# A fused attention and MLP kernel, forward and backward: the gradient over w1 for batch 0 moved from VectorE rows to TensorE columns, and the second pass begun two rows earlier

## The chip, the cores and the metric

The kernel runs on one core of one Trainium2 chip. The time is the device time of an execution in microseconds (us), the median of three runs. All matrices are bf16, and sums are kept in fp32.

## The reference, cut to what matters

One decode step of a transformer layer with a batch of two, and its gradient for every input:

```
x, grad_out: [2, 1, 640]     k_cache, v_cache: [2, 32, 4096, 128]
wq: [640, 4096]   wo: [4096, 640]   w1: [640, 1728]   w2: [1728, 640]

q  = layernorm(x) @ wq                      # 32 heads of 128
p  = softmax(q k^T * 128**-0.5);  o = p v
h  = x + o @ wo
h2 = h + relu(layernorm(h) @ w1) @ w2       # the output
outputs: h2, and the gradients of x, k_cache, v_cache, wq, wo, w1, w2 for grad_out
```

The caches are read, and gradients of their size are written: 64 K tiles and 64 V tiles of 1 MB come in, V comes in once more for the backward pass, and 128 tiles of 1 MB go out.

## The kernel before, in words

**Rows.** The program is written out by hand in one order (`tc.manual_schedule()`, L62): each engine executes its instructions in the order in which Python emits them. The outer loop (L1238) goes over `plan`; one iteration is called a row here, and row i handles pair i of 64 pairs (batch, head). H is 32, so rows 0 to 31 are batch 0.

**First pass.** `p1_iter(i)` (L468) is one row in eight steps k = 0 to 7: TensorE transposes the K tile of pair i (L440), scores come from one-column products (L453), the pair before it is scaled by its softmax weights on VectorE (`pk_half`, L486), and the V tile of the pair before that is multiplied (`m_part`, L476). So K tile i is read in rows i and i+1, V tile i in row i+2.

**Second pass.** `p2_iter(j)` (L884) makes the gradients of one pair's K and V and stores them, from a V tile called W. From row `P2_AT` on, every second row of the first pass carries one second-pass pair as well, and after row 65 only second-pass work is left. `P2_AT = H + 2 + M0_ITERS` (L1174); `M0_ITERS` is 7, so it is row 41. The first six pairs keep their V tile from the first pass.

**The middle.** Rows 34 to 40 lie between the end of batch 0's first pass and the first row of the second pass. There `middle_gen(0)` (L768) runs beside the first-pass rows of batch 1, as a generator that `bg_step` (L1155) advances by a credit in each step k. It needs the whole of batch 0 and yields what the second pass of batch 0 needs: the attention output through wo (`a_group`, L621), a layer norm, the 70 one-column products with w1 (`hf_ps`, L794), the gradient `ghfc` of the hidden values, and then the gradient over w1. For that, ghfc is spread over the partitions (`spread_some`, L655: a transpose for each chunk of 128 into PSUM and a copy on ScalarE), and VectorE multiplies and sums 15 pieces of w1 with it (`ttr`, L693, called at L816: five pieces of 640 columns, five of 640, five of 448). `turn()` (L699) lets at most five of these into a row. Then come the layer norm's gradient (`ln_bwd`) and the first heads of `go_group` (L708). In rows 34 to 40 `pk_act` (L491) also moves six of 32 scalings of a row to ScalarE.

**Loads.** All loads of the first pass stand in one list, `queue` (L1189), and go out in its order on SyncE's (SP's) DMA queue: K of row i, V of row i-2, and at rows named in `W_AT` (L1190) and `W2_AT` the four parts of wo, w1 (2160 KB, the fifth entry, row 35) and the three tiles of w2. `pump()` (L1205) is called in every step and issues as far as free buffers reach. A cache tile needs one of 13 buffers of 1 MB (`take("ld", ...)`, L90); each comes back with `give` when its tile has been read. w2's tiles hold buffers until `ga_gen` (L836) has used them, up to row 28. The last six pairs of batch 0 keep their V tile, so that from row 28 a row gives back one buffer and not two. w1 has a home of its own (`w1_t`, L343).

**The scratch around it.** `wide_row` (L648) is one row of 1280 columns that several steps use in turn. `later_heads()` (L651) is the part of the stored softmax weights that batch 1's last heads will fill, used as scratch until then. All small PSUM results share bank 7 (`mid`, `bc`, L71).

Of the kernel before, what the change touches and what calls it, by code (L numbers as in the profile page):

```python
# [7 lines left out]
FP32 = mybir.dt.float32  # L8
BF16 = mybir.dt.bfloat16
ALU = mybir.AluOpType  # L10
ACT = mybir.ActivationFunctionType
AX = mybir.AxisListType
# [3 lines left out]
def kernel(  # L16
# [20 lines left out]
    nc = tc.nc  # L37

    B, Sq, D = A_x.shape
    _, H, Sk, Dh = A_k_cache.shape  # L40
# [3 lines left out]
    ND = D // 128  # L44
# [3 lines left out]
    NF = NFF + (1 if F_rem else 0)  # L48
# [9 lines left out]
    def f_kc(c):  # L58
        return 128 if c < NFF else F_rem
# [7 lines left out]
    small = ctx.enter_context(tc.tile_pool(name="small", bufs=3))  # L67
# [5 lines left out]
    def pst(shape, dtype, role, name):  # L73

        k = banks[role].pop(0)
        banks[role].append(k)
        return ps.tile(shape, dtype, tag=f"bank{k}", bufs=1, name=name)
# [12 lines left out]
    def take(tag, shape, name):  # L90
        assert free[tag] > 0, (tag, name)
        free[tag] -= 1
        k = homes[tag].pop(0)
        stored.discard(k)
        t = pools[k].tile(shape, BF16, tag=f"big{k}", bufs=1, name=name)
        home_of[id(t)] = (tag, k, t)
        return t
# [9 lines left out]
    def give(t, to=None, out=False):  # L107
        tag, k, _ = home_of.pop(id(t))
        if out:
            stored.add(k)  # L110
        to = to or goes_to(tag)
        owned[tag] -= 1
        owned[to] += 1
        free[to] += 1
        homes[to].append(k)
        given_at[k] = step[0]
# [42 lines left out]
    ident_bf = const.tile([128, 128], BF16)  # L159
# [205 lines left out]
    FP = 6  # L365
# [51 lines left out]
    u4 = [None]  # L417
# [214 lines left out]
    def a_heads(i):  # L632

        if a_next[0] < o_next[0]:
            a_group()
        elif o_next[0] < NP1 // OG and i >= o_next[0] * OG + OG + 2:
            b, g = divmod(o_next[0], H // OG)
            if b > 0 or i >= W_AT[g * OG * 4 // H] + 4:
                o_group()
# [8 lines left out]
    def wide_row(name):  # L648
        return cols.tile([128, B * D], BF16, tag="wide_row", name=name)

    def later_heads():  # L651

        return P_bf[:, B * H - D // NSC:, :].rearrange("p h s -> p (h s)")

    def spread_some(colsrc, c0, n, kc_of, dst):  # L655

        t = pst([128, D], BF16, "bc", "bcb_ps")
        w = 0
        for c in range(c0, c0 + n):
            kc = kc_of(c)  # L660
            nc.tensor.transpose(t[:, w:w + kc], colsrc[0:kc, c:c + 1].to_broadcast([kc, 128]), ident_bf[0:kc, 0:kc])
            w += kc
        nc.scalar.copy(out=dst[:, 0:w], in_=t[:, 0:w])
        return w
# [19 lines left out]
    def store_rows(cols_bf, out_ap):  # L684
# [5 lines left out]
        nc.vector.tensor_copy(out=r[0:n, :], in_=t[0:n, :])  # L690
        nc.sync.dma_start(out=out_ap.rearrange("b s (c p) -> (b s c) p", p=128), in_=r[0:n, :])

    def ttr(in0, in1, acc, width, junk, kc=128):  # L693
        nc.vector.tensor_tensor_reduce(out=junk[0:kc, 0:width], in0=in0, in1=in1, scale=1.0, scalar=0.0,  # L694
                                       op0=ALU.mult, op1=ALU.add, accum_out=acc)
# [3 lines left out]
    def turn():  # L699

        while slot[0] <= 0:
            yield 0.0
        slot[0] -= 1

    def one(src, b):
        return src[:, :, b]
# [34 lines left out]
    def mlp_out():  # L741
# [23 lines left out]
        store_rows(y_bf, out_0)  # L765
        yield

    def middle_gen(b):  # L768
        if o_next[0] < (b + 1) * H // OG:
            o_group()  # L770
        u4[0] = wide_row("u")[:, 0:256].bitcast(FP32)
        nc.vector.tensor_reduce(out=u4[0], in_=u_bank[0][:].rearrange("p (s d) -> p d s", s=4),
                                axis=AX.X, op=ALU.add)
        yield
        while a_next[0] < (b + 1) * H // OG:
            if a_next[0] == o_next[0]:
                o_group()
                yield
                yield
            a_group()  # L780
            yield
        at_bf = small.tile([128, ND], BF16, tag="at_bf", bufs=1, name="at_bf")
        nc.vector.tensor_copy(out=at_bf[:], in_=asum[:, b, :])
        nc.vector.tensor_tensor(out=h1c[:, :, b], in0=xg32[:, b, :], in1=at_bf[:], op=ALU.add)
        h32 = small.tile([128, 1, ND], FP32, tag="h32", bufs=1, name="h32")
        nc.vector.tensor_copy(out=h32[:, 0, :], in_=h1c[:, :, b])
        yield ("a", b)
        u_out(b)
        yield from ln_fwd(h32[:], 1, x2c[:, :, b:b + 1], rstd2[:, b:b + 1])
        hf_ps = pst([128, NF], FP32, "mid", "hf_ps")  # L790
        for cf in range(NF):
            kc = f_kc(cf)
            for c in range(ND):
                nc.tensor.matmul(hf_ps[0:kc, cf:cf + 1], lhsT=w1_t[:, c, cf * 128:cf * 128 + kc],  # L794
                                 rhs=x2c[:, c, b:b + 1], start=(c == 0), stop=(c == ND - 1))
            yield 0.25
        nc.vector.tensor_scalar(out=acol[:, 0:NFF, b], in0=hf_ps[:, 0:NFF], scalar1=0.0, scalar2=None, op0=ALU.max)
        if F_rem:
            nc.vector.tensor_scalar(out=acol[0:F_rem, NFF, b:b + 1], in0=hf_ps[0:F_rem, NFF:NF],
                                    scalar1=0.0, scalar2=None, op0=ALU.max)  # L800
        mask = small.tile([128, NF], FP32, tag="mask", bufs=1, name="mask")
        nc.vector.tensor_single_scalar(out=mask[:], in_=acol[:, :, b], scalar=0.0, op=ALU.is_gt)
        nc.vector.tensor_tensor(out=ghfc[:, :, b], in0=ga[:, b, :], in1=mask[:], op=ALU.mult)
        yield from wait(3)
        fbc = wide_row("fbc")
        gx2 = small.tile([128, 1, ND], FP32, tag="gx2", bufs=1, name="gx2")
        gx2p = small.tile([128, ND, 3], FP32, tag="gx2p", bufs=1, name="gx2p")
        first_f = 0
        for k, n in enumerate((ND, ND, NF - 2 * ND)):
            row = fbc[:, (k % 2) * D:(k % 2 + 1) * D]  # L810
            w = spread_some(one(ghfc, b), k * ND, n, f_kc, row)
            yield
            for c in range(ND):
                yield from turn()
                part = w1_t[:, c, first_f:first_f + w]
                ttr(part, row[:, 0:w], gx2p[:, c, k:k + 1], w, part if b else later_heads())  # L816
                yield 0.85
            first_f += w
        nc.vector.reduce_sum(out=gx2[:, 0, :], in_=gx2p[:], axis=AX.X)
        yield ("w1", b)  # L820
        yield from ln_bwd(gx2[:], x2c[:, :, b:b + 1], rstd2[:, b:b + 1], gc[:, :, b:b + 1], gh1c[:, :, b:b + 1], 1)
        row = wide_row("hbc")
        hbc, junk = row[:, 0:D], row[:, D:2 * D]
        spread_some(one(gh1c, b), 0, ND, lambda c: 128, hbc)
        yield
        yield ("gh1", b)

        first = H - KEPT[b]
        bounds = [(first, first + 2), (first + 2, H)] if b == 0 else [(first, H)]
        bounds += [(h, min(first, h + GH)) for h in range(0, first, GH)]  # L830
        for h0, h1 in bounds:
            yield from go_group(b, h0, h1, hbc, junk)
        if b > 0:
            yield from mlp_out()
# [335 lines left out]
        forced[0] = False  # L1170

    EARLY = 2
    M0_ITERS = 7
    P2_AT = H + 2 + M0_ITERS  # L1174
    RATES = (0.2, 0.8, 0.2, 0.8, 0.45)
    RATE2 = 0.65
# [10 lines left out]


    queue = []  # L1189
    W_AT = (10, 15, 20, 24, 35)  # L1190
    W2_AT = (8, 13, 18)
    for n, (ii, jj) in enumerate(plan):
        if ii is not None:
# [11 lines left out]
    def pump():  # L1205
        while queue:
            what, k = queue[0]
            if what == "w":
                load_weights(k)
            else:  # L1210
                tag = "ld"
                if free["ld"] < 1 or (alone[0] and not ready("ld", 13)):
                    return
                if what == "w2":
                    w2_tiles[k] = load_w2(k, tag)
                else:
                    load_tile(what, k, tag)
            queue.pop(0)
# [19 lines left out]
    for n, (i, j) in enumerate(plan):  # L1238
# [57 lines left out]
        for k, _ in enumerate(p1_iter(i, i < H + 1, 0)):  # L1296
            for _ in range(at.get(k, 0)):
                if g2 is not None:
                    p2_step()
            if k == 5 and not H + 2 < i < P2_AT + 6:  # L1300
                a_heads(i)
            pump()

            spread[0] = 1 if i < P2_AT else 2
            at_k[0] = k
            if i >= P2_AT:
                slot[0] = int(k == 6 or (k == 1 and j is not None))
            elif i > H + 1:
                slot[0] = {1: 2, 3: 1, 4: 1, 6: 1}.get(k, 0)
            else:  # L1310
                slot[0] = int(k in (1, 6))
            bg_step(0, rate)
            bg_step(1, 0.0)
# [43 lines left out]
```

## Time and profile before

| | |
|---|---|
| median of 3 runs | 891.27 us (886.06 to 891.39) |
| profiled execution, its own time | 890.14 us |
| its span (first to last instruction) | 888.4 us |
| mean granted TensorE clock | 0.766 |
| busy: TensorE matmul, VectorE, ScalarE, GpSimd | 739.3, 680.5, 497.9, 170.9 us |
| moved by DMA | 361.86 MB, mean 407 GB/s over the span |
| read from HBM, written to it | 211.11 MB, 149.13 MB |
| a K or V tile from issue to landing, median | 17.3 us, 15.6 us |

The page cuts the span in 40 slices of 22.2 us; a digit is a share in tenths. A line of the view by windows names a stretch in us from the span's start, then its length, the busy time and instruction count of each engine in it, the granted clock of TensorE, the share of the 16 DMA engines' time in use, and the GB/s that they moved. PE is TensorE's matmul, PEld its weight loads, DVE is VectorE, ACT ScalarE, POOL GpSimd, SPq SyncE's DMA queue. In the profile w1 and w2 both appear under the name `w_t`, with the line telling them apart. The start of row i is the first K transpose of pair i on TensorE.

### The profile page before, as it was taken

Reading aid. Unit: us, or ns where it says so; the run is one execution under the profiler, and the core shown is the slowest. Engines: PE = TensorE matmul, PEld = TensorE weight load, DVE = VectorE, ACT = ScalarE, POOL = GpSimd, SP = SyncE. Lnnn points to the kernel's source line nnn. Section 1 sums busy time; section 2 is a strip of 40 time slices with the busy share of each in tenths; the row PEclk is TensorE's granted clock in tenths of the full one; section 3 lists DMA queues with packets and bytes.
Section 4 is the critical chain, followed back from the end, with each engine's and each line's share of the span. In section 5 each row is a group of like instructions: output and inputs, shape, how many; then the busy total and the mean of one; then the engine's idle time right before and its main releaser. Section 6 shows DMA issues by size and latency. Waiting matters only on the chain.

```text
span 888.4 us, 24848 instructions
## 1 busy us (share of the span) xinstructions
PE 739.3 (83%) x10143; PEld 618.9 (70%) x10143; DVE 680.5 (77%) x1281; ACT 497.9 (56%) x1292; POOL 170.9 (19%) x291
## 2 busy tenths in 40 slices
PE   4999899899999998987967887878876899967870
PEld 4887788789887887876757776656666667654550
DVE  2666788677788797885878898778878789989660
ACT  1444343345777665654635878777656766646660
POOL 1344433343212000000011101111001011211010
PEclk9999999899999998998995555555556755555655
DMA  9999999999879999999999999999999999999995
GB/s 379 425 419 415 417 409 417 426 423 388 312 301 401 418 422 426 422 425 426 421 392 394 416 422 424 425 425 425 426 425 411 424 425 414 425 427 424 424 424 230
DMA packets 56035, 361.86 MB, mean 407 GB/s; under 512 B 5681, under 2 KB 11505, under 8 KB 15217
## 3 DMA queue, kind: packets, MB, share of 16 engines
q1 hardware_dynamic: 46968, 303.29, 82.4%
q0 software_dynamic: 8912, 56.97, 15.6%
q8 instruction: 80, 1.31, 0.5%
q14 instruction: 35, 0.28, 0.1%
q10 hardware_dynamic: 40, 0.01, 0.0%
HBM read 211.11 MB, written 149.13 MB: 406 GB/s over the span
## 4 chain that ended last, share of the span: by engine, by line
PE 36%; DMA 32%; DVE 16%; ACT 9%; issue 4%; SPq 0%; DVEq 0%; ACTq 0%; POOL 0%; POOLq 0%
PE t_ps L440 15%; DMA Vt<-in_A_v_cache_dram 13%; DMA out_dram<-gV 12%; PE m_ps L476 9%; DMA out_dram<-gK 6%; DVE gK L860 5%; ACT gV L950 4%; DVE gV L860 4%; PE s_ps L453 3%; DVE pk L486 3%; PE u_ps L514 2%; ACT t_sb L445 2%; PE dp_ps L453 2%; DMA Kt<-in_A_k_cache_dram 2%; DVE hbc L694 2%
## 5 line engine op out<-in xcount | busy, mean ns | idle before, releaser
L445 ACT COPY t_sb<-t_ps 128x512 f32<-128x512 f32 x479 | 273.0, 587 | 197.3 <-PE t_ps L440 193.0
L453 PEld LDWEIGHTS <-t_sb 128*128 128x128 bf16 x4096 | 179.7, 103 | 57.9 <-ACT t_sb L445 30.4
L440 PE MATMUL t_ps<-ident_f,Wt 128*128 128x128 f32 x832 | 199.9, 391 | 1.5 <-ACT t_sb L445 1.5
L486 DVE TENSOR_TENSOR pk<-Kt,ep 128x2048 bf16<-128x2048 bf16 (+1 forms) x128 | 152.7, 1193 | 49.1 <-ACT ep L540 30.6
L476 PE MATMUL m_ps<-pk,Vt 128*128 128x129 bf16 x2048 | 172.4, 223 | 20.6 <-DMA Vt<-in_A_v_cache_dram 19.4
L860 DVE TENSOR_TENSOR gK<-rb,gsp 128x2048 bf16<-128x2048 bf16 x128 | 152.9, 1223 | 20.9 <-DMA out_dram<-gV 16.4
L476 PEld LDWEIGHTS <-Vt 128*128 128x128 bf16 x2048 | 125.9, 99 | 51.7 <-issue 29.0
L440 PEld LDWEIGHTS t_ps<-ident_f,Wt 128*128 128x128 f32 x832 | 138.9, 203 | 29.8 <-issue 21.8
L440 PE MATMUL t_ps<-ident_f,Kt 128*128 128x128 f32 x1024 | 154.8, 284 | 3.8 <-DMA Kt<-in_A_k_cache_dram 3.2
L860 DVE TENSOR_TENSOR gV<-rb,pp 128x2048 bf16<-128x2048 bf16 (+1 forms) x128 | 143.2, 1144 | 18.5 <-DMA out_dram<-gV 13.3
L440 PEld LDWEIGHTS t_ps<-ident_f,Kt 128*128 128x128 f32 x1024 | 113.0, 144 | 6.4 <-ACT t_sb L445 2.7
L502 POOL COPY pk<-ep 128x16 bf16<-128x16 bf16 x80 | 84.5, 1058 | 160.9 <-ACT ep L540 79.3
L453 PE MATMUL dp_ps<-gom,t_sb 128*128 128x2 bf16 x2048 | 96.3, 168 | 19.6 <-ACT t_sb L445 19.1
L453 PE MATMUL s_ps<-qm,t_sb 128*128 128x2 bf16 x2048 | 87.4, 164 | 1.5 <-DVE t_sb L443 1.5
L1004 ACT CAST ot<-o_ps 128x512 bf16<-128x512 f32 (+3 forms) x152 | 67.4, 492 | 6.7 <-PE o_ps L998 4.2
L604 ACT CAST MT<-m_ps 128x128 bf16<-128x128 f32 x64 | 17.0, 265 | 95.2 <-PE m_ps L476 95.1
L905 POOL COPY pp<-P_bf 128x64 bf16<-128x64 bf16 x64 | 34.1, 536 | 127.7 <-DVE gV L860 125.0
L903 ACT ACTIVATE rb<-dp_ps,rt 128x256 bf16<-128x256 f32 x64 | 30.2, 472 | 42.3 <-PE dp_ps L898 41.5
L694 DVE CUSTOM_DVE_ANT_0 hbc<-wo_t,hbc 128x640 bf16<-128x640 bf16 x64 | 52.8, 826 | 0.3
L694 DVE CUSTOM_DVE_ANT_0 gxj<-wqs,gqr 128x1024 bf16<-128x1024 bf16 x40 | 48.8, 1220 | 0.2
L950 ACT ACTIVATE gV<-rb,pa 128x128 bf16<-128x128 bf16 x152 | 46.5, 394 | 0.0
L440 PE MATMUL t_ps<-ident_f,Vt 128*128 128x128 f32 x192 | 40.4, 351 | 1.8 <-ACT t_sb L445 1.8
(208 smaller groups left out, 710.7 us busy)
## 6 DMA issues: line engine op xcount, KB each, us to landing
Kt<-in_A_k_cache_dram SPq DMA_DIRECT2D x64, 1024.0 KB, 17.3
Vt<-in_A_v_cache_dram SPq DMA_DIRECT2D x64, 1024.0 KB, 15.6
Wt<-in_A_v_cache_dram SPq DMA_DIRECT2D x52, 1024.0 KB, 17.0
out_dram<-gK SPq DMA_DIRECT2D x48, 1024.0 KB, 17.4
out_dram<-gV SPq DMA_DIRECT2D x47, 1024.0 KB, 17.9
out_dram<-gV POOLq DMA_DIRECT2D x17, 1024.0 KB, 9.7
out_dram<-gK POOLq DMA_DIRECT2D x16, 1024.0 KB, 10.2
wq_t<-in_A_wq_dram SPq DMA_DIRECT2D x5, 1024.0 KB, 6.8
```

The costliest lines, as they stand in the source:

```text
L440: nc.tensor.transpose(t_ps[:, j, :], natf[:, 2 * cc:2 * cc + 2, :].rearrange("p c k -> p (c k)"), ident_f[:])
L445: nc.scalar.copy(out=t_sb[:], in_=t_ps[:])
L453: nc.tensor.matmul(dst[:, sc:sc + 2], lhsT=v[:, j, :, par], rhs=vecs[:, par, :], start=(par == 0), stop=(par == 1))
L476: nc.tensor.matmul(r["m"][:, 0:129], lhsT=r["V"][:, sc, :], rhs=r["pk"][sc // HALF][:, sc % HALF, 0:129], start=(sc == 0), stop=(sc == NSC ...
L486: nc.vector.tensor_tensor(out=p["pk"][k][:, 0:n, 0:128].rearrange("p s (a two) -> p s a two", two=2), in0=p["K"][:, sl, :].rearrange("p s ...
L502: nc.gpsimd.tensor_copy(out=col, in_=e)
L694: nc.vector.tensor_tensor_reduce(out=junk[0:kc, 0:width], in0=in0, in1=in1, scale=1.0, scalar=0.0, op0=ALU.mult, op1=ALU.add, accum_out=acc)
L860: nc.vector.tensor_tensor(out=pairs_view(dst[:, sl, :]), in0=row.rearrange("p (a two) -> p a two", two=2)[:, None, :, :].to_broadcast([128 ...
L903: nc.scalar.activation(out=rb[:], in_=bank[:, 128:384], func=ACT.Copy, scale=rt[:, b, h:h + 1])
L905: nc.gpsimd.tensor_copy(out=pp[:], in_=P_bf[:, b * H + h, :, None].to_broadcast([128, NSC, 2]))
L950: nc.scalar.activation(out=gV[:, NSC - act + k, :], in_=c["rb"][:, 0:128], func=ACT.Copy, scale=pa[:, k:k + 1])
L1004: nc.scalar.copy(out=ot[0:P, k, n0:n0 + nn], in_=o_ps[0:P, 0:nn])
```

## The change

Four things are done together.

1. **w1 is loaded at row 12.** The fifth entry of `W_AT` becomes 12. Since loads run ahead, its DMA is issued behind K tile 12 and V tile 10, in row 7.
2. **w1 is transposed on TensorE.** From row 14 on, at the end of a row (k = 7), `w1_transpose` takes one of w1's 14 chunks of 128 hidden columns: five 128x128 transposes into bank 7 and one copy of 640 columns on ScalarE. Chunks 0 to 5 and 6 to 11 go to two of the 13 `ld` buffers (taken in rows 14 and 20), chunk 12 to `later_heads()` and chunk 13 to a `wide_row`; these last two wait until `ga` is done and come in rows 29 and 30.
3. **Batch 0's gradient over w1 is 70 one-column products** (`gx_by_chunks`) with the transposed w1, summed in PSUM; the two `ld` buffers are then given back, in row 36. Batch 1 keeps the old way (`gx_by_rows`, the removed lines moved there).
4. **`M0_ITERS` is 5.** The middle is rows 34 to 38, and the second pass begins at row 39.

```diff
+    w1T = {"next": 0, "tiles": []}
+    def w1T_chunk(cf):
+        if cf < 2 * FP:
+            return w1T["tiles"][cf // FP][:, cf % FP, :]
+        return later_heads() if cf == 2 * FP else w1T["row"][:, D:2 * D]
+    def w1_transpose():
+        cf = w1T["next"]
+        if cf >= 2 * FP:
+            if "ga" not in done:
+                return
+            if cf > 2 * FP:
+                w1T["row"] = wide_row("u")
+        elif cf % FP == 0:
+            w1T["tiles"].append(take("ld", [128, FP, D], "w1T"))
+        kc = f_kc(cf)
+        t = pst([128, D], BF16, "mid", "w1T_ps")
+        for c in range(ND):
+            nc.tensor.transpose(t[0:kc, c * 128:(c + 1) * 128], w1_t[:, c, cf * 128:cf * 128 + kc], ident_bf[:])
+        nc.scalar.copy(out=w1T_chunk(cf)[0:kc, :], in_=t[0:kc, :])
+        w1T["next"] = cf + 1
+    def gx_by_chunks(b, gx2):
+        t = pst([128, ND], FP32, "mid", "gx_ps")
+        for c in range(ND):
+            for cf in range(NF):
+                kc = f_kc(cf)
+                nc.tensor.matmul(t[:, c:c + 1], lhsT=w1T_chunk(cf)[0:kc, c * 128:(c + 1) * 128],
+                                 rhs=ghfc[0:kc, cf, b:b + 1], start=(cf == 0), stop=(cf == NF - 1))
+            yield 0.5
+        for w in w1T["tiles"]:
+            give(w)
+        nc.vector.tensor_copy(out=gx2[:, 0, :], in_=t[:])
...
-        for k, n in enumerate((ND, ND, NF - 2 * ND)):
-            row = fbc[:, (k % 2) * D:(k % 2 + 1) * D]
-            w = spread_some(one(ghfc, b), k * ND, n, f_kc, row)
-            yield
-            for c in range(ND):
-                yield from turn()
-                part = w1_t[:, c, first_f:first_f + w]
-                ttr(part, row[:, 0:w], gx2p[:, c, k:k + 1], w, part if b else later_heads())
-                yield 0.85
-            first_f += w
+        if b == 0:
+            yield from gx_by_chunks(b, gx2)
+        else:
+            yield from gx_by_rows(b, gx2)
...
-    M0_ITERS = 7
+    M0_ITERS = 5
+    W1T_AT = 14
...
-    W_AT = (10, 15, 20, 24, 35)
+    W_AT = (10, 15, 20, 24, 12)
...
+            if k == 7 and W1T_AT <= i < H and w1T["next"] < NF:
+                w1_transpose()
```

## The prediction

> **What bounds the kernel now.** I read the page's slices first, then the view by windows cut at the rows, then SyncE's and TensorE's timelines around the middle.
>
> ```profile
> PEclk9999999899999998998995555555556755555655
> DMA  9999999999879999999999999999999999999995
> GB/s 379 425 419 415 417 409 417 426 423 388 312 301 401 418 422 426 422 425 426 421 392 394 416 422 424 425 425 425 426 425 411 424 425 414 425 427 424 424 424 230
> ```
>
> DMA is full in nearly every slice. The bytes, 361.86 MB, are the same after the change, so the time moves only with DMA time that is left unused. Apart from start and tail there is one large hole: slices 10 to 13 (388, 312, 301, 401), the middle. Cut at the rows (first line rows 12 to 25, second rows 26 to 33, third rows 34 to 42):
>
> ```profile
> 81.07:169.52 88.45, 80.85 (x1370) 70.08 (x1367) 67.44 (x134) 33.64 (x102) 33.20 (x44) 0.96 1.02 416
> 169.52:212.64 43.12, 43.12 (x763) 38.18 (x760) 32.35 (x59) 18.93 (x58) 19.31 (x23) 1.00 1.01 422
> 212.64:271.28 58.64, 57.63 (x984) 50.80 (x981) 48.27 (x138) 44.73 (x132) 14.21 (x33) 0.97 0.83 316
> ```
>
> Rows 12 to 25 take 6.3 us each and TensorE has 7.6 us to spare in them: they wait for tiles. Rows 26 to 33 have TensorE busy throughout, 5.4 us each. In rows 34 to 42 DMA moves 316 GB/s against 423 when full: 58.64 x (1 - 316/423) = 14.8 us are lost there. Row by row (34 to 42):
>
> ```profile
> 212.64:218.88 6.24, 6.24 (x121) 5.78 (x118) 5.08 (x20) 4.67 (x15) 2.51 (x6) 1.00 0.90 363
> 218.88:226.04 7.16, 7.16 (x166) 6.51 (x162) 4.87 (x19) 4.96 (x17) 1.91 (x6) 1.00 0.97 363
> 226.04:233.29 7.25, 7.25 (x100) 6.52 (x97) 4.09 (x12) 4.93 (x13) 1.71 (x4) 0.76 0.71 293
> 233.29:238.79 5.50, 5.50 (x100) 4.88 (x97) 5.43 (x13) 4.89 (x15) 1.42 (x4) 1.00 0.70 253
> 238.79:244.96 6.17, 5.87 (x99) 4.88 (x97) 6.10 (x17) 4.97 (x17) 2.02 (x4) 1.00 0.90 340
> 244.96:251.03 6.07, 5.92 (x103) 5.12 (x100) 5.32 (x19) 5.10 (x18) 1.14 (x4) 1.00 0.96 368
> 251.03:257.09 6.06, 5.91 (x101) 5.15 (x98) 5.21 (x16) 4.91 (x14) 1.52 (x5) 1.00 0.91 341
> 257.09:265.56 8.47, 8.11 (x137) 7.15 (x134) 7.80 (x19) 5.26 (x14) 0.70 (x1) 1.00 0.52 204
> 265.56:271.28 5.72, 5.67 (x103) 4.82 (x100) 4.39 (x9) 5.03 (x16) 1.26 (x1) 1.00 1.01 352
> ```
>
> Engines, not DMA, set these rows: TensorE is busy for almost all of each, VectorE for 5.43 of 5.50 and 6.10 of 6.17 us in rows 37 and 38, where most of the 15 pieces lie. A row of the first pass asks for two tiles of 1.05 MB, 4.96 us at 423 GB/s, and takes 5.5 to 7.3 us.
>
> SyncE's timeline shows what fills part of that hole now: w1.
>
> ```profile
> 202.08 0.43 SPq L363 DMA_DIRECT2D w_t<-in_B_w_dram  x1
> 208.06 0.33 SPq L461 DMA_DIRECT2D Kt<-in_A_k_cache_dram  x1
> 212.81 0.33 SPq L461 DMA_DIRECT2D Vt<-in_A_v_cache_dram  x1
> 218.97 0.33 SPq L461 DMA_DIRECT2D Kt<-in_A_k_cache_dram  x1
> ```
>
> It goes out at 202.08, when loads have already thinned to one tile in 5 to 6 us (208.06, 212.81, 218.97), because the kept V tiles hold buffers. So w1's 2.21 MB travel almost free of charge.
>
> **The change part by part.** The end of the hole is a state: the row from which DMA is full again, row 43 before (420 GB/s), row 41 after. By the built program's order both have the same K and V tiles asked for relative to the row, so the changed kernel reaches it with two rows' loads, 4.19 MB, not yet made. These cost 4.19/0.423 = 9.9 us later, where DMA is full. The result is therefore: change of row 34's start, plus the time of rows 34 to 40 after, minus the 58.64 us, plus 9.9 us.
>
> *w1 at row 12.* It now travels among rows 12 to 25, which wait for tiles, and holds each later tile back by 2.21 MB: 2.21/0.423 = 5.2 us. It is issued behind K tile 12 and V tile 10 on SyncE, and K tile 13 and all behind it wait. The end of that stretch is a V tile's landing (row 25 lasts 9.76 us for it), so row 26 starts 5.2 us later; rows 26 to 33 are TensorE's and keep their length. Bounds: 0, if the later rows make it up (K tile 34 lands 8.9 us before row 34), and 5.3 at 416 GB/s. I take 5.2, since lead that row 26 lacks can't shorten TensorE-bound rows.
>
> *70 transposes, 14 copies.* No transpose of w1 is in the trace; the nearest are five 128x128 bf16 ones before a copy:
>
> ```profile
> 229.50 0.61 PE L661 MATMUL bcb_ps<-ident_bf,ghfc 128*128 128x128 bf16 x5
> 229.95 0.40 PE L476 MATMUL m_ps<-pk,Vt 128*128 128x129 bf16 x4
> ```
>
> The next matmul starts 0.45 us after them, so 0.45 us per chunk. Twelve chunks (5.4 us) fall in rows 14 to 25, under TensorE's 7.6 us of waiting plus 5.2 us that w1 adds; without this cover they would cost up to 5.4 us. Two fall in rows 29 and 30: +0.9 us. The copies (0.69 us each, as L663's) are ScalarE work beside 33.64 busy of 88.45 us: nothing; a copy late in a row can hold the next row's transposes by some 0.3 us, under the same cover. Bank 7 is shared with `a_group`, whose sum VectorE reads within its row: nothing.
>
> *Two `ld` buffers fewer, rows 14 to 36.* A tile goes out one row closer to its use. In the built order K tile 36 and V tile 34 leave at the end of row 34 and are read from row 36's start; before, the same tiles left two rows or more ahead. The lead is row 35 (about 7.2 us) for K and about 7.7 us for V. The landings of these stretches:
>
> ```profile
> DMA to landing us min/median/max: 6.4/13.0/16.5
> ...
> DMA to landing us min/median/max: 7.2/8.3/15.2
> ```
>
> (K from 186 to 262 us, V from 190 to 290 us.) Where the queue is nearly empty I take the lower ends, so rows 36 and 37 wait 0 to 0.6 us for V; 0 in the sum, the rest in the range. In row 36 two buffers come back at once and four loads leave together.
>
> *70 products for 15 pieces.* The twin of the new products is L794:
>
> ```profile
> 223.19 0.89 PE L794 MATMUL hf_ps<-x2c,w_t 128*128 128x1 bf16 x30
> 223.94 0.63 PE L476 MATMUL m_ps<-pk,Vt 128*128 128x129 bf16 x8
> ```
>
> 30 in 0.75 us before the next starts, 25 ns each: 70 cost TensorE 1.8 us, in row 36. Removed there are five spread transposes (0.45 us) and later nine more, three copies, and on VectorE 10 x 0.82 + 5 x 0.62 = 11.3 us:
>
> ```profile
> L694 DVE CUSTOM_DVE_ANT_0 P_bf<-w_t,fbc x15: 608/812/840, 230.9 to 247.2; 128x640 bf16<-128x640 bf16 x10, 128x448 bf16<-128x448 bf16 x5
> ```
>
> Rows 37 and 38 thus fall from VectorE to TensorE's own pace.
>
> *Rows 34 to 40 after.* Row 34 and 35 as now, 6.24 and 7.16. Row 36: 5.4 us (a row that TensorE sets) plus 1.8 for the products, nothing for a cold clock (0.76 in row 36 now): 7.2. Row 37: layer norm's gradient and one spread, 5.4 + 0.5 = 5.9. Row 38: the first two heads, as row 40 now, 6.0. Rows 39 and 40, the first of the second pass, as 41 and 42 now, 8.47 and 5.72. Sum 46.7. Bounds: 40.2 with the five middle rows at the shortest row, 5.21; 49.9 with rows 36 to 38 at 7.25 each.
>
> *Sum.* 5.2 + 0.9 + 46.7 - 58.64 + 9.9 = +4.1 us on the profiled execution's 890.14: 894.2. That execution lies 1.1 us under the median, less than the runs differ among themselves; I give 894. Afterwards nothing gets shorter: the second pass moves the same bytes at 420 to 427 GB/s.
>
> **The rivals.**
>
> *A. w1 stays hidden.* Row 34 starts as now, because lead over TensorE makes the 5.2 us up. For it: rows 26 to 33 wait for no tile. Against: TensorE is the limit in them, so they can't run faster to make anything up. It gives 894.2 - 5.2 = 889.0, still within 1%; with the middle rows at their floor too (46.7 to 40.2), 882.5. That is about the most that the middle can give.
>
> *B. The two buffers are missed* (slower by over 1%). Place: V tiles of rows 36 and 37, one row ahead. It sets in when a V tile takes over 7.7 us to land; at 11.5 us (between 8.3 and the 15.2 that a full queue showed) two rows wait 3.8 us each, 7.6 in all, 901.8; at 15.2 it is 15 us, 909. The limit of 900.2 is crossed from about 10.7 us. For it: landings over 13 us are common in this stretch. Against: those belong to a queue with many tiles in it, and here two would be in it. The Trainium skill, "DMA: Bandwidth & Descriptors", section "Anatomy of one DMA", gives 2.0 us plus bytes over 436 GB/s for one DMA (on GpSimd's path; these leave from SyncE): by that a tile lands in 4.4 us and B can't occur. The trace does not agree, its shortest K landing here is 6.4 us, so B keeps a chance.
>
> *C. The middle doesn't fit in five rows*, and the first second-pass row runs what is left in one lump. By the built order both first heads are done in row 38, so this doesn't happen; were one row short, it costs about a row, 6 us: 900.
>
> **How the numbers follow.** About 1% (8.9 us) is what a measurement of this kernel can tell from no change: 882.4 to 900.2 counts as within 1%. The forecast, a loss of some 4 us between -1 and +8: 0.56. A: 0.22, of which half its way to the floor, 0.11, is faster by over 1% or at its edge. B: 0.17, and C with unforeseen waits 0.05; of these 0.20 end over 900.2. So faster 0.11, within 1% 0.69, slower 0.20. The range leaves out the last of A and the far half of B: 882 to 905. The likeliest case alone: 889 to 898.
>
> **What would show it.** Row 34 starts 5 to 6.5 us later than 212.64. Rows 34 to 40 take 44 to 49 us. GB/s before row 34 sinks earlier, in rows 31 to 33, since w1 no longer fills them. Rows 14 to 25 show TensorE busier and no longer than w1's bytes explain. V waits in rows 36 and 37 are under 1 us. I am wrong if row 34 keeps its start (A), or if TensorE waits for V or K for several us between rows 28 and 38 (B).

## The result, and the profile after

The changed kernel takes 900.47 us (899.76 to 903.64, 4 runs) and the kernel before 889.43 us beside it (886.06 to 891.39): the ratio on record is 1.0144 with an interval of 1.0106 to 1.0181. The two medians alone give 1.0124, 11.0 us; against the medians of the kernel before in the later experiments (888.0 and 887.4 us) it is 1.0140 and 1.0147. So the change makes the kernel slower by 1.2 to 1.5%. The number forecast was 894; 900.5 lies in the range of 882 to 905, above the 889 to 898 of the likeliest case, and it is slower by over 1%, to which the prediction gave 0.20. The profiled execution took 900.28 us, 10.1 more than the one before.

The page's slices after, as they stood for the kernel before:

```profile
PEclk9999899999799999999997555555656855565555
DMA  9999999996869999999999999999999999999996
GB/s 379 425 418 416 414 411 417 421 423 235 336 246 396 424 423 425 423 427 423 426 418 390 397 414 425 425 425 424 426 422 399 426 422 403 419 424 425 425 423 269
```

The hole is still in slices 10 to 13, and deeper: 235, 336, 246, 396 where 388, 312, 301, 401 stood. Cut at the rows (rows 12 to 25, 26 to 33, 34 to 40; columns as in the prediction):

```profile
81.12:172.62 91.50, 84.30 (x1430) 73.58 (x1428) 67.73 (x135) 40.53 (x115) 34.27 (x44) 0.96 1.02 416
172.62:216.61 43.99, 43.99 (x771) 38.85 (x767) 32.26 (x59) 20.50 (x60) 19.32 (x23) 1.00 0.92 377
216.61:270.96 54.35, 51.72 (x871) 46.18 (x867) 37.45 (x117) 34.35 (x101) 12.06 (x26) 0.91 0.73 274
```

Rows 12 to 25 last 91.50 us in place of 88.45, still with DMA full. Rows 26 to 33 last 0.87 us longer, and DMA sinks to 377 GB/s in them. The seven rows up to the state in which DMA is full again take 54.35 us; the prediction had 46.7. One by one, from row 32 to row 40:

```profile
205.98:211.39 5.41, 5.41 (x97) 4.79 (x94) 3.03 (x6) 2.29 (x8) 1.66 (x3) 1.00 0.74 298
211.39:216.61 5.22, 5.22 (x96) 4.60 (x93) 3.28 (x5) 2.88 (x9) 2.37 (x2) 1.00 0.60 207
216.61:222.86 6.25, 6.25 (x121) 5.78 (x118) 5.09 (x20) 4.68 (x15) 2.51 (x6) 1.00 0.51 174
222.86:230.06 7.20, 7.20 (x166) 6.55 (x162) 4.87 (x19) 4.96 (x17) 1.91 (x6) 0.99 0.84 309
230.06:241.56 11.50, 11.50 (x166) 10.41 (x164) 3.72 (x13) 4.73 (x14) 1.33 (x4) 0.65 0.73 286
241.56:249.83 8.27, 7.06 (x101) 6.21 (x102) 5.52 (x18) 5.29 (x15) 1.92 (x4) 0.88 0.89 355
249.83:255.67 5.84, 5.46 (x95) 4.78 (x95) 5.26 (x18) 4.51 (x14) 2.32 (x5) 1.00 0.94 358
255.67:265.04 9.37, 8.38 (x139) 7.44 (x138) 8.41 (x22) 4.94 (x12) 0.70 (x1) 1.00 0.33 117
265.04:270.96 5.92, 5.87 (x106) 5.01 (x103) 4.58 (x10) 5.23 (x16) 1.37 (x2) 1.00 1.03 368
```

Two rows stand out: row 36 with 11.50 us and a granted clock of 0.65, row 37 with 8.27 us and 0.88. TensorE is busy without a gap in row 36, and VectorE for 3.72 of its 11.50 us: the row is TensorE's, at a lower clock. The clock's steps, cut from 229.89 us on:

```profile
229.89:233.30 3.41, 3.41 (x25) 3.33 (x25) 1.08 (x6) 1.48 (x4) 0.17 (x1) 0.50 0.93 372
233.30:236.71 3.41, 3.41 (x85) 3.25 (x84) 0.63 (x1) 0.89 (x2) 0.81 (x2) 1.00 0.56 228
236.71:243.54 6.83, 6.83 (x74) 5.90 (x74) 2.86 (x11) 2.95 (x10) 0.34 (x2) 0.50 0.80 306
```

Both stretches at 0.50 in this cut follow a stretch of one-column products: the 70 of `hf_ps` (row 35), then the 70 new ones. TensorE's timeline shows the new ones and what comes behind them (start, duration, instruction):

```profile
236.15 0.44 PE L723 MATMUL gx_ps<-ghfc,w1T 128*128 128x1 bf16 x12
...
237.19 1.04 PE L514 MATMUL u_ps<-pk,hot 128*32 128x512 bf16 x8
...
245.88 0.62 PE L514 MATMUL u_ps<-pk,hot 128*32 128x512 bf16 x8
```

The same eight products take 1.04 us at 237.19 and 0.62 us a row later. The new products themselves run from 233.69 to 235.23 and from 236.15 to 237.19, 2.58 us in place of the 1.8 forecast.

The view of waits, TensorE's, rows 26 to 38: no tile is waited for, and there is a new wait, at the end of row 37.

```profile
PE d_ps L761 <- DVE gom L356: 1.2, 1, 1.2
PE pr_ps L351 <- DVE goc L754: 0.4, 1, 0.4
```

### The profile page after: what moved, and what is told of

It is laid out like the page before. It is cut to its first block, busy times and chain, and to the rows that moved or that the text cites. A ratio compares the mean times of both kernels' runs of the same rounds, so it can differ in the third digit from the quotient of the medians.

```text
span 898.4 us, 25033 instructions
## 1 busy us (share of the span) xinstructions
PE 744.7 (83%) x10269; PEld 622.5 (69%) x10269; DVE 673.3 (75%) x1253; ACT 498.8 (56%) x1287; POOL 169.7 (19%) x284
## 4 chain that ended last, share of the span: by engine, by line
PE 36%; DMA 35%; DVE 13%; ACT 8%; issue 6%; SPq 0%; ACTq 0%; DVEq 0%; POOL 0%; POOLq 0%
DMA Vt<-in_A_v_cache_dram 17%; PE t_ps L440 15%; DMA out_dram<-gV 9%; PE m_ps L476 8%; DMA Wt<-in_A_v_cache_dram 4%; DVE gV L904 3%; ACT gV L994 3%; PE s_ps L453 3%; ACT t_sb L445 3%; DVE gK L904 3%; PE u_ps L514 2%; DVE pk L486 2%; DMA out_dram<-gK 2%; PE dp_ps L453 2%; DVE gxj L731 2%
## 5 line engine op out<-in xcount | busy, mean ns | idle before, releaser
L440 PE MATMUL t_ps<-ident_f,Wt 128*128 128x128 f32 x832 | 196.6, 386 | 1.1 <-ACT t_sb L445 1.1
L440 PE MATMUL t_ps<-ident_f,Kt 128*128 128x128 f32 x1024 | 157.3, 287 | 5.0 <-DMA Kt<-in_A_k_cache_dram 4.1
L440 PEld LDWEIGHTS t_ps<-ident_f,Wt 128*128 128x128 f32 x832 | 136.4, 200 | 28.2 <-issue 19.6
L904 DVE TENSOR_TENSOR gV<-rb,pp 128x2048 bf16<-128x2048 bf16 (+1 forms) x128 | 143.7, 1146 | 15.4 <-DMA out_dram<-gV 10.1
L994 ACT ACTIVATE gV<-rb,pa 128x128 bf16<-128x128 bf16 x144 | 44.0, 392 | 0.0
L918 DVE SCALAR_TENSOR_TENSOR gsp<-dp_ps,negdot,P_bf 128x64 bf16<-128x64 f32 x64 | 17.9, 280 | 34.1 <-PE dp_ps L453 34.1
## 6 DMA issues: line engine op xcount, KB each, us to landing
out_dram<-gK POOLq DMA_DIRECT2D x17, 1024.0 KB, 10.1
```

Of the source, the lines that this page charges most:

```text
L440: nc.tensor.transpose(t_ps[:, j, :], natf[:, 2 * cc:2 * cc + 2, :].rearrange("p c k -> p (c k)"), ident_f[:])
L904: nc.vector.tensor_tensor(out=pairs_view(dst[:, sl, :]), in0=row.rearrange("p (a two) -> p a two", two=2)[:, None, :, :].to_broadcast([128 ...
L994: nc.scalar.activation(out=gV[:, NSC - act + k, :], in_=c["rb"][:, 0:128], func=ACT.Copy, scale=pa[:, k:k + 1])
```

## The experiments

The theory after this reading has two separate losses: w1's bytes, moved from the hole to rows where DMA is full, and TensorE's clock, halved after the one-column products. Its main rival is that the two load buffers held by the transposed w1 starve the rows. Each kernel was timed beside runs of the kernel before, so each ratio is to that one.

### 1. Only the early load

```diff
-    W_AT = (10, 15, 20, 24, 35)
+    W_AT = (10, 15, 20, 24, 12)
```

> The kernel before with one edit: w1 is loaded at row 12, everything else as before. Theory (w1's 2.21 MB are paid for where DMA is full, rows 12 to 25, and no longer fill the hole of the middle): row 34 starts 3 to 5 us later, rows 34 to 42 keep their 58.6 us, the time rises by 3 to 5 us over the kernel before. Rival (rows 26 to 33 make it up, w1 was never worth anything in the hole): within 1 us of before.

Measured: 894.26 against 888.0 us, ratio 1.0069 (1.0047 to 1.0091). Rows 12 to 25, 26 to 33 and 34 to 42 in its profile:

```profile
81.23:172.40 91.17, 81.00 (x1371) 69.87 (x1367) 67.38 (x134) 33.74 (x103) 33.20 (x44) 0.96 1.02 416
172.40:215.51 43.11, 43.11 (x762) 38.17 (x759) 32.33 (x59) 18.92 (x57) 19.32 (x23) 1.00 1.00 418
215.51:272.62 57.11, 56.10 (x984) 49.37 (x982) 48.19 (x138) 44.54 (x132) 15.35 (x33) 1.00 0.81 307
```

Rows 12 to 25 are 2.7 us longer than before, rows 26 to 33 equal within a hundredth: nothing is made up. Row 34 starts 2.9 us later, just under the 3 to 5 expected. Rows 34 to 42 did not keep their 58.6 us, they take 57.11: in this execution the clock stayed at 1.00 behind `hf_ps`, and row 36 lasts 5.71 us in place of 7.25. The profiled execution took 891.48 us, the least of its six; the median lies 6 us over before. Early w1 alone is about half of the loss; the time is above the 3 to 5 us expected.

### 2. Transposes without the early load

w1 at row 35 again; the transposes read wo.

```diff
-    W_AT = (10, 15, 20, 24, 12)
+    W_AT = (10, 15, 20, 24, 35)
...
-            nc.tensor.transpose(t[0:kc, c * 128:(c + 1) * 128], w1_t[:, c, cf * 128:cf * 128 + kc], ident_bf[:])
+            nc.tensor.transpose(t[0:kc, c * 128:(c + 1) * 128], wo_t[:, c, (cf % ND) * 128:(cf % ND) * 128 + kc], ident_bf[:])
```

> The changed kernel with w1 loaded at row 35 again; the 70 transposes keep their place, number and shape but read columns of wo, so batch 0's gradient over w1 is made of the wrong numbers and what follows from it is not the reference's. Theory (early w1 costs 4 to 5 us of the 11): 4 to 5 us under the changed kernel, about 896, row 34 starting within 1 us of the kernel before. Rival (the two buffers that the transposed w1 holds are the loss): no change, 900.

Measured: 898.31 us, ratio 1.0116 (1.0091 to 1.0142). Row 34 starts at 211.61 us, 5.0 earlier than in the changed kernel, as the theory says, but the time falls by only 2 us, between what the theory (896) and the rival (900) said. With two buffers fewer w1 leaves SyncE at 212.15 us, and row 35 waits for it:

```profile
PE hf_ps L848 <- DMA w_t<-in_B_w_dram: 1.2, 1, 1.2
```

Row 35 takes 9.3 us and not 7.2, part of it at 0.50 of the clock. The run spoils its own question; run 9 asks it again.

### 3. Wide products between the one-column products

```diff
-        t = pst([128, ND], FP32, "mid", "gx_ps")
+        t = pst([128, 512], FP32, "mid", "gx_ps")
...
+            nc.tensor.matmul(t[:, 8:512], lhsT=ident_bf[:], rhs=w1_t[:, c, 0:504], start=True, stop=True)
             yield 0.5
...
```

> The changed kernel with one wide product (504 columns, result unused) behind each 14 one-column products of the gradient, five in all, some 0.2 us each. Theory (a stretch of one-column products makes the granted clock halve, 6.8 us at 0.5 from 236.5 us on, which costs about 3.4 us in rows 36 and 37): the second stretch at 0.5 goes or shrinks, rows 36 and 37 together 2 to 3 us shorter than 19.8, the time about 898. Rival (the products and the waits around them are long by themselves): rows 36 and 37 1 us longer, about 901.

Measured: 898.89 us, ratio 1.0125 (1.0105 to 1.0144). Rows 36 and 37:

```profile
229.91:239.66 9.75, 9.48 (x172) 7.96 (x169) 3.18 (x12) 4.54 (x14) 1.33 (x4) 1.00 0.71 267
239.66:246.97 7.31, 6.10 (x103) 5.30 (x102) 5.77 (x20) 5.29 (x17) 1.93 (x4) 1.00 1.02 426
```

The clock is 1.00 in both, and they take 17.1 us and not 19.8, although five products of 0.22 us were added. So the halved clock, both stretches together, was worth 2.7 + 1.1 = 3.8 us in the changed kernel's profile. The stretch behind `hf_ps` is also gone, though nothing was added there: that one comes and goes between executions. The rival is refuted for these two rows. That the wide products kept the clock up behind the new ones is not shown: the products also lie otherwise in the windows of 3.41 us in which the clock changes (counted in the section on the prediction). In the end-to-end time the gain, 1.6 us, is within the intervals; in the profile row 41 starts 2.9 us earlier than in the changed kernel (268.10 for 270.96), but the span ends only 0.5 us earlier, and where the rest is lost was not traced.

### 4. The second pass from row 41 again

```diff
-    M0_ITERS = 5
+    M0_ITERS = 7
```

> The changed kernel with the second pass from row 41 again, all else as changed. Theory (a row of the middle without background work takes about 5.8 us for loads worth 4.96, so two more rows cost 11.6 and save 9.9): 1 to 2 us over the changed kernel, about 902. Rival (beginning the second pass two rows earlier is itself the loss, since it comes before its loads are ready): 895 or less.

Measured: 904.89 us, ratio 1.0193 (1.0172 to 1.0215), 4.4 us over the changed kernel. The two rows more (39 and 40) are one window:

```profile
255.76:271.00 15.24, 12.05 (x201) 10.22 (x199) 13.93 (x43) 9.18 (x28) 2.87 (x9) 1.00 0.78 283
```

15.24 us for loads worth 9.9: VectorE is busy for 13.93 us of it, with products of further heads that otherwise lie under the second pass. In the kernel before, the same two rows lasted 12.13 us (6.07 and 6.06 in the prediction's view), with two of these head products and not eight. So the earlier start helps the changed kernel by 4.4 us, but about 3 us of that is work which the changed kernel itself had moved into the two rows; the time is also above the 902 expected.

### 5. Only the two buffers

The kernel before, with two buffers taken in rows 14 and 20 and given back in row 36.

```diff
+    held = []
...
+            if (i, k) in ((14, 7), (20, 7)):
+                held.append(take("ld", [128, FP, D], "held"))
+                nc.gpsimd.memset(held[-1][:, 0, 0:2], 0.0)
+            if (i, k) == (36, 4):
+                for t in held:
+                    give(t)
```

> The kernel before, with two of the 13 load buffers taken out of use in rows 14 and 20 and given back in row 36, as the transposed w1 takes them, and nothing else. Theory (the shorter lead empties the DMA queue earlier, but no row waits for a tile for more than about 0.3 us): row 43 starts within 1 us of the kernel before, and so does the end. Rival (the lost lead is a large part of the 11 us): TensorE waits for K or V tiles in rows 28 to 38 and the time rises by 4 us or more.

Measured: 890.12 against 887.4 us, ratio 1.0026 (1.0012 to 1.0040). This lies between the two: row 43 starts 0.7 us later, as the theory says, but the median ends 2.7 us later. Yet the only wait of TensorE for a DMA between 186 and 240 us is not for a tile, but for w1, which again leaves later (211.17 us).

```profile
PE hf_ps L794 <- DMA w_t<-in_B_w_dram: 1.3, 1, 1.3
```

DMA falls to 225 GB/s in row 33 here (321 in row 32) without any row getting longer for it. The rival, and with it the prediction's rival B, is refuted as a large part of the loss.

### 6. The one-column products spread out

```diff
                                  rhs=ghfc[0:kc, cf, b:b + 1], start=(cf == 0), stop=(cf == NF - 1))
-            yield 0.5
+            yield 1.6
```

> The changed kernel with the five sets of 14 one-column products handed out one in every second step and not three and two at once; no work is added. Theory (it is the density of one-column products that lets the granted clock halve): the stretch at 0.5 that begins at 236.5 us goes or halves, rows 36 and 37 lose 2 to 3 us, and since the middle ends some steps later, up to 1 us comes back in rows 38 and 39: about 898.5. Rival (the clock falls for another reason there): clock and time as in the changed kernel, 900 to 901.

Measured: 895.0 us, ratio 1.0086 (1.0063 to 1.0110), 5.5 us under the changed kernel and more than expected. Rows 36 and 37:

```profile
230.66:239.71 9.05, 9.03 (x150) 8.07 (x148) 3.20 (x9) 4.73 (x14) 1.33 (x4) 0.82 0.56 232
239.71:245.70 5.99, 5.99 (x106) 5.34 (x106) 2.81 (x8) 4.14 (x12) 2.23 (x4) 1.00 0.86 330
```

The second stretch at 0.50 is gone (0.82 in row 36 is the one behind `hf_ps`), the wait for `gom` too, since the heads' products come later, and row 39 takes 8.3 us and not 9.4: 5.1 us in rows 36 to 40. So the gain is the clock and the moved work together; the run does not part them.

### 7. Two parts of wo later, in the kernel before

```diff
-    W_AT = (10, 15, 20, 24, 35)
+    W_AT = (10, 15, 26, 29, 35)
```

> The kernel before with the last two of wo's four parts (1.31 MB each) asked for at rows 26 and 29 and not at 20 and 24. Theory (bytes that rows 11 to 25 do not have to wait for are worth their time at 420 GB/s, the mirror image of the early w1): row 26 starts 4 to 6 us earlier and the time falls by 3 to 6 us, to 882 to 885. Rival (only the place of the wait moves, to rows 26 to 34): within 1 us of the kernel before.

Measured: 886.07 against 887.4 us, ratio 0.9987 (0.9972 to 1.0001): no difference that can be told, and not the theory's 3 to 6 us. Rows 12 to 25 and 26 to 33:

```profile
81.35:162.34 80.99, 77.10 (x1351) 67.63 (x1348) 66.55 (x131) 33.65 (x103) 31.81 (x43) 1.00 1.02 417
162.34:208.12 45.78, 43.72 (x763) 38.14 (x759) 32.99 (x60) 18.93 (x58) 20.05 (x26) 1.00 1.02 420
```

Row 26 starts 7.2 us earlier, and rows 26 to 33 give 2.7 us back (45.78 for 43.12), 2.0 of it in waits for tiles. The median gains less than this profile. A likely reason, not shown, is that the profile of the kernel before holds a stretch at 0.50 in row 25 (clock 0.65, 9.76 us) that other executions need not have.

### 8. wo later and wide products, in the changed kernel

```diff
-    W_AT = (10, 15, 20, 24, 12)
+    W_AT = (10, 15, 24, 29, 12)
...
+            if cf % 2:
+                nc.tensor.matmul(hf_ps[:, 16:512], lhsT=ident_bf[:], rhs=w1_t[:, 0, 0:496], start=True, stop=True)
             yield 0.25
...
```

with the wide products of run 3 as well.

> The changed kernel with wo's last two parts at rows 24 and 29 and with wide filler products among the one-column products of both kinds (seven among the 70 of the forward product with w1, five among the gradient's). Theory (early w1 and the halved clock are two separate losses, and the move of wo gives back 1.31 to 2.6 MB, 3 to 6 us): 893 to 896. Rival (the place of the loads before row 26 is worth nothing): 898 to 900, what the fillers alone bring.

Measured: 898.93 us, ratio 1.0133 (1.0107 to 1.0158): the rival's figure. The move of wo lets row 34 start at 214.86, 1.75 us earlier, and the fillers in row 35 take it back (9.0 us for 7.2). The clock is at 1.00 in all of the middle, but fillers cost their own time, which spreading does not.

### 9. The spread version without the early load

The edits of runs 2 and 6, but w1 at row 33, so that it lands in time:

```diff
-    W_AT = (10, 15, 20, 24, 12)
+    W_AT = (10, 15, 20, 24, 33)
```

> The changed kernel with the spread products of the run before (one set of 14 in every second step) and, as in the second run, transposes that read wo, with w1 loaded at row 33, so that it lands before row 35 (batch 0's gradient over w1 and what follows from it are not the reference's). Theory (early w1 costs the 5 us by which row 34 starts later): row 34 at 211 to 212 us and no row waiting for w1, 4 to 5 us under the spread version's 895.0, so about 890.5. Rival (what is loaded in rows 12 to 25 is given back elsewhere): within 1.5 us of 895.

Measured: 889.57 against 888.0 us, ratio 1.0015 (1.0002 to 1.0029), 5.4 us under run 6. Row 34 starts at 211.34 us and not 217.24. Rows 36 and 37 at full clock:

```profile
224.96:232.75 7.79, 7.55 (x150) 6.74 (x148) 3.19 (x9) 4.64 (x14) 1.33 (x4) 1.00 0.63 261
232.75:238.74 5.99, 5.99 (x106) 5.33 (x106) 2.81 (x8) 4.14 (x12) 2.23 (x4) 1.00 0.90 335
```

These are close to the 7.2 and 5.9 us of the prediction; the stretch behind `hf_ps` did not come in this execution. With both losses taken away, the kernel is within 1.6 us of the kernel before: the rest of the change, transposes, buffers, new products and shorter middle, about cancels out. What each of these is worth in this run was not measured.

### 10. The spread version with the second pass from row 41

```diff
-    M0_ITERS = 5
+    M0_ITERS = 7
```

> The spread version with the second pass from row 41 again. Theory (each middle row costs 5.8 us or more for loads worth 4.96, and the heads' products that would lie under the second pass are pulled into them): 2 to 5 us over the spread version, 897 to 900. Rival (the earlier start is worth nothing or harms): 895 or less.

Measured: 900.54 us, ratio 1.0130 (1.0105 to 1.0155), 5.5 us over run 6. Its profiled execution took 904.25 us, the most of its six, and shows that spreading is no guarantee; row 36:

```profile
229.93:241.32 11.39, 11.15 (x150) 9.71 (x147) 3.20 (x9) 4.74 (x14) 1.33 (x4) 0.53 0.49 186
```

Up to row 38 its program is that of run 6, yet the clock stayed at 0.50 from the stretch behind `hf_ps` through the new products. So a part of the 5.5 us may be the clock; with run 4's 4.4 us the earlier start is worth some 4 to 5 us to the changed kernel.

### 11. One part of wo later, in the kernel before

```diff
-    W_AT = (10, 15, 20, 24, 35)
+    W_AT = (10, 15, 20, 28, 35)
```

> The kernel before with only wo's last part moved, from row 24 to row 28. Theory (1.31 MB leave rows 11 to 25, worth 3.1 us at 420 GB/s, and rows 26 to 34 have enough lead to take them without a wait, which two parts did not have): 884 to 886 and no waits for tiles after row 26. Rival (the wait only moves): 887 to 888, as before.

Measured: 886.61 against 888.0 us, ratio 0.9979 (0.9963 to 0.9996). Rows 12 to 25 and 26 to 33:

```profile
81.18:164.56 83.38, 78.09 (x1371) 68.06 (x1367) 67.19 (x134) 33.67 (x103) 32.21 (x44) 1.00 1.02 417
164.56:207.79 43.23, 43.23 (x762) 38.10 (x759) 32.60 (x59) 18.95 (x57) 19.70 (x24) 1.00 1.02 420
```

Rows 26 to 33 keep their length and wait for nothing, as expected, and the kernel beats both by a little: 1.4 us, less than the 3.1 expected.

## Why the prediction was right and wrong

Its sum, term by term, against the profiled execution:

| term | predicted, us | measured, us |
|---|---|---|
| row 34's start | +6.1 (5.2 for w1, 0.9 for two chunks) | +3.97 |
| rows 34 and 35 | 13.4 | 13.45 |
| row 36 | 7.2 | 11.50 |
| row 37 | 5.9 | 8.27 |
| row 38 | 6.0 | 5.84 |
| rows 39 and 40 | 14.19 | 15.29 |
| less the rows 34 to 42 before | -58.64 | -58.64 |
| the loads left | +9.9 | +10.3 |
| sum | +4.1 | +10.0 (the runs differ by 10.1) |

The loads left are measured as what remains of the span: from row 41 on in the changed kernel 898.4 - 270.96 = 627.4 us, from row 43 on in the kernel before 888.4 - 271.28 = 617.1. So this accounting by rows and loads was off by only 0.4 us.

**w1 at row 12: right.** With and without the early load the same program starts row 34 5.0 us (changed kernel and run 2) and 5.9 us (runs 6 and 9) apart; 5.2 was the term, and run 9 puts 5.4 us on the end. Rival A is refuted by run 1. The difference of 3.97 to the kernel before is smaller because of that profile's row 25:

```profile
159.76:169.52 9.76, 8.47 (x109) 7.02 (x110) 4.72 (x9) 1.96 (x5) 2.72 (x3) 0.65 1.01 428
```

The prediction put its 9.76 us down to a V tile's landing. TensorE was idle for only 1.29 of them, and 6.83 us at 0.50 of the clock lie in the row: an accident of one execution that the sum took for a property. In run 5, with the same loads and no such stretch there, row 34 starts at 210.62 us, 2.0 earlier, and the changed kernel's 216.61 is then 6.0 later.

**Transposes: right.** Rows 29 and 30 are 0.8 us longer together (5.49 and 5.73 for 5.22 and 5.21), the others lie in rows that wait for tiles. Runs 2 and 5 differ up to row 34 in the transposes alone: row 26 starts at 167.62 and 167.50 us, so the twelve earlier chunks cost next to nothing, and row 34 at 211.61 and 210.62. From the first of a chunk's five to the next matmul it is 0.27 us (0.40 for the last chunk) where 0.45 was assumed.

**The two buffers: right for the tiles.** No tile is waited for in rows 26 to 38, and DMA sank in rows 31 to 33, as said, at no cost to the rows. K tile 36 landed 4.8 us after its issue, faster than any K tile in the prediction's stretch (6.4). Run 5's 0.26% (0.12 to 0.40%) is not nothing, as the sum had it, but it holds a wait for w1, which early w1 doesn't have.

**The products and row 36: wrong, and this is the step that failed.** The prediction put the row at "5.4 us (a row that TensorE sets) plus 1.8 for the products, nothing for a cold clock (0.76 in row 36 now): 7.2". The 0.76 stood in the prediction's own fence, behind the 70 products of `hf_ps`, and was taken for something of that row, when the change was to put 70 more products of the same kind there. No rival named the clock. Of the 6.7 us by which rows 36 and 37 exceed their terms, 3.8 are the clock (by run 3, both stretches at 0.50), 0.8 the products' own length (2.58 for 1.8), 1.2 the wait of `d_ps` for `gom` behind VectorE's long product; the last 0.9 were not traced. Run 9, at full clock and with the head products later, has 13.8 us in these two rows against the 13.1 of the prediction.

**The clock rule.** The Trainium skill, "TensorE: Matmul & The Clock Gate", section "Part 1: The HAM clock gate", says that the clock is passed at half or full rate according to how busy the array was in a free-running window of 3413 ns. The trace agrees with the window: around the middle the stretches at 0.50 last 3.41, 6.83 or 13.65 us, all multiples of 3.41, and the clock is never anything between 0.5 and 1.0. The rule of the same page of the Trainium skill, section "Why this matters for your kernels", to leave no idle gaps of over 3 us between matmuls would not have warned here: TensorE was busy for 7.20 of 7.20 us in row 35, ahead of the first fall, and for 3.41 of 3.41 us ahead of the second.

**Where the products lie in the window.** The steps of the clock in one execution lie on one grid of 3.41 us, and the place of the grid differs from execution to execution. The view by windows of the products alone, between two lines of the grid, gives the length, TensorE's busy time and (x) products, VectorE's, then clock, DMA and GB/s. The first four lines are `hf_ps` in the kernel before, the changed kernel, run 1 and run 9; the last is the new products in the changed kernel:

```profile
223.07:226.48 3.41, 2.29 (x70) 0.23 (x2) 1.00 1.01 368
226.48:229.89 3.41, 2.09 (x69) 0.00 (x0) 1.00 0.99 389
224.70:228.11 3.41, 1.53 (x50) 0.00 (x0) 1.00 1.01 428
221.02:224.43 3.41, 1.70 (x57) 0.00 (x0) 1.00 1.00 420
233.31:236.72 3.41, 2.18 (x59) 0.00 (x0) 1.00 0.56 228
```

Behind the first, second and last line the clock is at 0.50, behind the third and fourth it stays at 1.00. All kept traces divide like this. Where one window held 67 or more of the 70 of `hf_ps`, the clock fell (before, after, runs 4, 6, 10); where the grid divided them so that the fuller window held 40 to 57, it did not (runs 1, 3, 7, 8, 9, 11). It fell behind 59, 69 and 64 of the new products (after, runs 4 and 2) and not behind 54, 28, 42 and 42 (runs 3, 6, 8, 9). In runs 2 and 5 it fell behind fewer of `hf_ps`, but there TensorE had waited over 1 us for w1 in the window. So the same products cost the clock or not by where the grid lies: the changed kernel and run 3 have one program up to there, and 69 and 50 of `hf_ps` in the fuller window. Run 3's 54 is below the 57 that run 9 had without any wide product, so run 3 does not show that wide products are a cure. Spreading keeps the count low: 28 in run 6, 42 in run 9.

**M0_ITERS: the sign was right.** Runs 4 and 10 put two rows more at 4.4 and 5.5 us; the prediction's accounting, rows against loads, gave the direction.

**The range: right in part by luck.** 900.47 us lies within 882 to 905, but the upper end was held open for rival B, the missing buffers, which run 5 refutes as a large loss. The 54.35 us of rows 34 to 40 lie outside the bounds that the prediction gave them, 40.2 to 49.9 (the upper one adds up to 49.3 from its own terms: 13.4 + 21.75 + 14.19). Of the signs that it named, row 34 (3.97 us later, not 5 to 6.5) and rows 34 to 40 (54.35 us, not 44 to 49) failed; the GB/s before row 34, the busier TensorE in rows 14 to 25 and the missing waits for tiles came as said.

What stays open: no run moved the products by a part of a window on purpose, so the count rests on comparing executions, one profile for each kernel. Wide products as a cure, and a cure for the wait of `d_ps`, were not put to a test of their own.

## What to carry to other kernels

Where DMA is full, count in bytes: a load moved out of a hole into a full stretch costs its bytes over the full rate (2.21 MB, 5 us), whatever it does for the code around it. Before many one-column products go to TensorE, look at the granted clock behind those already there, and spread them so that few lie in any 3.4 us. A sum against one profiled execution inherits its accidents, so look at the clock column before a row is taken as a measure.

## What the runs showed of the hardware

TensorE's granted clock was 0.50 or 1.00 and changed on a grid of 3.41 us. With TensorE busy throughout, it fell behind windows in which 59 or more one-column products of a group began (2.18 us of busy time of 3.41 in the changed kernel, with the fall at 236.71 us) and stayed at 1.00 behind windows with 57 or fewer (1.70 us in run 9). With the sets a step apart it stayed in runs 6 and 9; in run 10, where it was low when they began, it was at 0.50 for four windows with 13 to 18 of them each. One-column products cost 25 ns each for `hf_ps` and 37 ns each for the new ones (42 in 1.54 us), a difference that no run explains.
